# A two-stage mixer kernel on one core: second weights' high parts on ScalarE, a third staging buffer with loads two ahead, sums in pieces, first norm transposes later

## The chip, the cores and the metric

The kernel runs on 1 core of a Trainium2 chip. The metric is the device time of one execution in microseconds, lower is better.

## The reference

Per head (8 x 8 heads, 576 rows, 64 columns) an attention without scores: softmax of q along its columns, softmax of k along the rows, `kv = k_s^T v`, `q_s kv`. The heads are put side by side to x [8, 576, 512]. Then two stages:

```
u   = x + (relu(x^T w_tok1) w_tok2)^T          # mixing along the rows
x1  = u + relu(u w_ch1) w_ch2                  # w_ch1 512x1536
xn  = (x1 - mean) / sqrt(var + 1e-6) * g_ln    # per row
out = x1 + relu(xn w2_ch1) w2_ch2              # w2_ch1 512x2048
```

The weights come in as 64-bit floats; the kernel takes them as pairs of 32-bit words and decodes them on the chip.

## The kernel before, in words

**Precision.** Each operand of a large matmul is split into a high part (rounded to fp32r) and a low part, and each product is three matmuls (`PASSES`: high-high, high-low, low-high).

**Blocks.** The 4608 rows are nine blocks of 512 (`NB`). Blocks 0 to 7 are the first 512 rows of each batch entry; block 8 gathers the remaining 64 rows of each (the row ends), which go through `u_dram` (`load_ends`, L641). Phase 1 (`Phase1`, L647) computes x1 block by block: twelve steps `f` of 128 hidden columns, each `L1` (12 matmuls into `ph`, L675), the relu split (`relu_split`, L140: high part on ScalarE, low part on VectorE) and, two steps later (`LAG`), `L2` (12 matmuls into the accumulators `acc`, L692). Phase 2 (`Phase2`, L800) does the same for the normalised rows with sixteen steps (L814, L829). There are two `ph` buffers.

**Order of the work.** It is written out by hand. `later(n, fn)` (L308) puts a function n ticks ahead, `tick()` (L311) issues what is due. In phase 1 a step has four ticks (in the middle and at the end of L1 and of L2), in phase 2 two. Within an engine's queue the order is that of issue.

- Attention units (`Unit`, L401) of the next batch entry run beside phase 1 of blocks 2 to 6, each unit 10 ticks after the one before. POOL does the subtractions of k and q, the scaling of q and the low part of q (`q_split`, L507, tile `qn`), which `tok1` (L533, tile `pg`) multiplies.
- At a block's end `Phase1.finish` (L699) adds acc and the high part of u on VectorE (L713) and the low part of u on POOL, one instruction over the whole tile yT (L715). `y_store` (L619) transposes a quarter of it (tile `py`, L622) 5, 7, 9 and 11 ticks later, copies it on ScalarE (L632) and stores it to `y_dram` from ScalarE's DMA queue.
- `Norm(j)` (L728) loads a block of y from `y_dram` (`load_y`, L722, SP queue; its tile shares a buffer with that of the y stores), takes statistics (L753), normalises (`hat`, L778) and from 12 ticks on transposes (`turn`, tile `px`, L789) into xT. `Norm(0)` starts at tick 18 of block 8 of phase 1, `Norm(1)` at tick 14 of block 0 of phase 2.

**Weights.** `Loads` (L259) holds chunks of 512 KB, a load (SP queue) and a use. `decode` (L87) gives the use's steps: `rebias` (L100), `shift` (L108), `sign` (L115), `low` (L121), all on VectorE for the second weights (`late`), then `parts`: the high part by a copy on VectorE (L129) and the low part by a subtraction on POOL (L130). `pump` issues so many of these steps; the load of a later chunk stands between the `parts` of one chunk and the `rebias` of the next. The last argument but one of `Loads` is how many chunks are loaded ahead. The 32 chunks of the second weights start with block 7 of phase 1 (eight chunks, into the pool `w2pool`, which takes the place of the attention's tiles) and run on to the last steps of block 0 of phase 2, whose step f needs chunks up to 4(f // 2) + 2 and, for L2, + 4. They come through two staging buffers, given out by `stage` (L148): an entry of -1 in `extra` is one of the two main buffers, another the entry of `bufs`.

Of the kernel before, what the change touches and what calls it, by code (L numbers as in the profile page):

```python
# [8 lines left out]
F32 = mybir.dt.float32  # L9
# [15 lines left out]
def kernel(  # L25
# [61 lines left out]
    def decode(st, w, hi, lo):  # L87


        rows, n = st.shape[0], st.shape[1]  # L90
        w0, w1 = st[:, :, 0], st[:, :, 1]
        wf = w1.bitcast(F32)
        vec, late = nc.vector, bool(w2p)
        box = {}
        if late:
            box["t"] = main.tile([P, 512], U32, tag="t", bufs=2, name="t")[:rows, 0:n]

        def rebias():
            if late:
                vec.tensor_scalar(out=wf, in0=wf, scalar1=REBIAS, scalar2=None, op0=ALU.mult)  # L100
            else:
                nc.scalar.activation(out=wf, in_=wf, func=AF.Copy, scale=REBIAS)

        def shift():
            if not late:

                box["t"] = psum("dt").bitcast(U32)[:rows, 0:n]
            vec.tensor_scalar(  # L108
                out=box["t"], in0=w1, scalar1=3, scalar2=0x7FFFFFF8,
                op0=ALU.logical_shift_left, op1=ALU.bitwise_and,  # L110
            )

        def sign():
            t = box["t"]
            vec.scalar_tensor_tensor(  # L115
                out=t, in0=w1, scalar=0x80000000, in1=t, op0=ALU.bitwise_and, op1=ALU.bitwise_or
            )

        def low():
            t = box["t"]  # L120
            vec.scalar_tensor_tensor(  # L121
                out=t if late else w0, in0=w0, scalar=29, in1=t,
                op0=ALU.logical_shift_right, op1=ALU.bitwise_or,
            )

        def parts():
            x = w((box["t"] if late else w0).bitcast(F32))
            if late:
                vec.tensor_copy(out=hi, in_=x)  # L129
                nc.gpsimd.tensor_tensor(out=lo, in0=x, in1=hi.bitcast(F32), op=ALU.subtract)  # L130
            else:
                split(x, hi, lo, nc.gpsimd)

        return [rebias, shift, sign, low, parts]
# [173 lines left out]
    def later(n, fn):  # L308
        ticks.setdefault(now[0] + n, []).append(fn)
# [91 lines left out]
    class Unit:  # L401
# [7 lines left out]
        def start(self, at):  # L409
            steps = (  # L410
                self.k_max, self.k_top, self.q_max, self.q_sub, self.k_sub, self.q_exp,
                self.q_norm, self.k_exp, self.q_split, self.kv, self.tok1,
                lambda: self.q_T(0), self.hidden, lambda: self.q_T(1),
                lambda: self.tok2(0), lambda: self.tok2(1),
            )
            if self.n == 0:
                later(at + 10, lambda: loads.until(3))
                later(at + 14, lambda: loads.until(len(tok)))
            if self.early:
                when = (0, 1, 1, 1, 3, 3, 4, 5, 7, 8, 10, 10, 11, 12, 14, 15)  # L420
            else:
                when = (0, 2, 1, 2, 4, 4, 5, 6, 8, 8, 10, 11, 13, 12, 15, 16)
            for n, fn in zip(when, steps):
                later(at + n, fn)
# [194 lines left out]
    def y_store(j, c):  # L619
        pt = psum("py")  # L620
        for kk in range(KD):
            nc.tensor.transpose(  # L622
                out=pt[:, kk * P:(kk + 1) * P], in_=yT_t[j][:, kk, c * P:(c + 1) * P],
                identity=ident,
            )
        if w2p:
            if c == 0:
                yn_t[j] = w2p[0].tile([P, CT, DM], F32, tag="y", name="yn")
            yn = yn_t[j][:, c]
        else:  # L630
            yn = main.tile([P, DM], F32, tag="t", bufs=2, name="yn")
        nc.scalar.activation(out=yn, in_=pt[:, 0:DM], func=AF.Copy)  # L632
        if j < B:
            dst = y_dram[j * S:j * S + S0, :].rearrange("(p c) d -> c p d", c=NC)[c]
            nc.scalar.dma_start(out=dst, in_=yn)
            return
        for i in range(P // R):
            b = c * (P // R) + i
            nc.scalar.dma_start(out=y_dram[b * S + S0:(b + 1) * S, :], in_=yn[i * R:(i + 1) * R])
# [7 lines left out]
    class Phase1:  # L647
# [51 lines left out]
        def finish(self):  # L699
            if self.f1 < NF1:  # L700
                t = [main.tile([P, 512], F32, tag="t", bufs=2, name="part") for _ in range(2)]
                x = att.tile([P, 2, 512], F32, tag="qx", name="part")
                for dd, o in enumerate((t[0], t[1], x[:, 0], x[:, 1])):
                    nc.scalar.activation(out=o, in_=self.acc[dd], func=AF.Copy)
                for dd in range(2):
                    nc.sync.dma_start(out=part_dram[:, dd], in_=t[dd])
                nc.sync.dma_start(out=part_dram[:, 2:4], in_=x)
                return
            yT_t[self.j] = main.tile([P, KD, BLK], F32, tag="y", bufs=1, name="yT")
            yT, u = yT_t[self.j], u_t[self.j]  # L710
            for dd in range(KD):
                x = self.part[dd // 2][:, dd % 2] if self.f0 else u[:, 0, dd].bitcast(F32)
                nc.vector.tensor_tensor(out=yT[:, dd], in0=self.acc[dd], in1=x, op=ALU.add)  # L713
            if self.f0 == 0:
                nc.gpsimd.tensor_tensor(out=yT, in0=yT, in1=u[:, 1].bitcast(F32), op=ALU.add)  # L715
            for c in range(CT):
                later(5 + 2 * c, lambda c=c: y_store(self.j, c))


# [8 lines left out]
    class Norm:  # L728
        def __init__(self, j):
            self.j = j  # L730

        def start(self, at):
            def call(fn, i):
                return lambda: fn(i)

            later(at, self.load)
            for i in range(CT // 2):
                later(at + 4 + i, call(self.stats, i))
                later(at + 9 + i, call(self.hat, i))
            later(at + 6, self.root)  # L740
            later(at + 8, self.rstd)
            for kk in range(KD):
                later(at + 12 + kk + kk // 2, call(self.turn, kk))

        def load(self):
            self.y = load_y(self.j, w2p[0])
# [99 lines left out]
    with tc.manual_schedule():  # L846
# [89 lines left out]
        for o, f in steps:  # L936
            if isinstance(o, Phase1):
                if o.j == 1 and f == NF1 - 2:
                    for hp in range(NHP):
                        Unit(2 * NHP + hp).start(OFF + 1 + hp * GAP)  # L940
                    later(7, part.load_part)
                if f == 0:
                    if 1 < o.j < B - 1:
                        for hp in range(NHP):
                            Unit((o.j + 1) * NHP + hp).start(OFF + hp * GAP)
                    elif o.j == B - 1:
                        att.release()
                        w2pool = tc.alloc_tile_pool(name="w2pool", bufs=1, reuse_waits="tile")
                        pool_bufs[w2pool] = 4
                        w2p.append(w2pool)  # L950
                        extra.clear()
                        loads = Loads([
                            x
                            for g in range(NF2 // 2)
                            for x in ch_chunks(
                                wa2, w2_ch1, wb2, w2_ch2, g, w2pool if g < 2 else main
                            )
                        ], 1, 1, 8)
                        for n in range(5, 29):
                            later(n, lambda: loads.pump(2))  # L960
                        later(10, load_ends)
                    elif o.j == NB - 1:
                        Norm(0).start(18)
                if o.j <= 1:
                    loads.until(len(tok) + 4 * (f // 2) + 2)
            else:
                if o.j == 0:
                    loads.until(4 * (f // 2) + 2)
                if f == 0:
                    later(16, o.load)  # L970
                    if o.j + 1 < NB:
                        Norm(o.j + 1).start(14 if o.j == 0 else 8)
            ps, n = o.L1(f, tick)
            h = main.tile([P, 2, 512], F32R, tag="h", bufs=LAG + 1, name="h")
            relu_split(ps, h[:, 0, 0:n], h[:, 1, 0:n])
            tick()
            loads.pump(rate(7, 2, 3))
            pend.append((o, f, h))
            if len(pend) > LAG:
                do_L2()  # L980
                loads.pump(rate(4, 3, 4))
                tick()
# [34 lines left out]
```

## Time and profile before

| | |
|---|---|
| median of 3 runs | 1693.29 us (1693.03 to 1695.51) |
| the profiled execution | 1692.61 us, its span 1690.8 us |
| granted TensorE clock, mean | 0.998 of full speed |
| TensorE busy (matmuls) | 1650.4 us, 98% |
| VectorE busy | 665.7 us, 39% |
| ScalarE busy | 393.8 us, 23% |
| POOL busy | 314.2 us, 19% |

How to read it: times in the trace count from the start of the span. A row of the timeline has start, duration, engine, line, operation, output and inputs, how many instructions are merged, and in brackets the idle time before and what ended it. Phase 1 reaches block 7 near 726 us and block 8 near 800 us, phase 2 starts at 868 us. ACT is ScalarE, DVE VectorE, PE TensorE, POOL GpSimd, SPq the DMA queue of SyncE.

### The profile page before, as it was taken

The page shows a single profiled execution, that of the slowest core. Times are in us where ns is not written, and L with a number is a line of the kernel's source. Part 1 is how long each engine was busy: PE and PEld are TensorE (multiplying, and loading weights), DVE is VectorE, ACT ScalarE, POOL GpSimd, SP SyncE. Part 2 cuts the span into 40 slices and gives each one's busy share as a digit, 9 for nine tenths or more (in the row PEclk, how much of TensorE's full clock was granted, in tenths as well). Part 3 has the DMA queues.
Part 4 walks back from the last instruction along what each step waited for, and adds up shares of the span by engine and source line. Part 5 has one row for each costly group of instructions (what it writes and reads, how often), then busy time and mean ns, then how long its engine had stood idle before and what let it go on. Part 6 is the DMA issues. An engine that isn't in the chain of part 4 may idle for free.

```text
span 1690.8 us, 20156 instructions
## 1 busy us (share of the span) xinstructions
PE 1650.4 (98%) x8136; PEld 1379.6 (82%) x8136; DVE 665.7 (39%) x1322; ACT 393.8 (23%) x792; POOL 314.2 (19%) x220
## 2 busy tenths in 40 slices
PE   5999999999999999999999899999999999999998
PEld 4888888888888888888788788888888888888887
DVE  6875434343433434354567722222213122222211
ACT  4663323333232323311211111111111111111110
POOL 5744522232222313221222200000000000000000
PEclk9999999999999999999999999999999999999999
DMA  8452312122121212042225310101010102010010
GB/s 228 124 169 67 98 33 74 43 56 50 38 67 30 71 38 74 21 144 63 88 63 174 100 51 25 50 25 50 25 51 25 50 1 75 1 53 23 0 50 25
DMA packets 122062, 105.39 MB, mean 62 GB/s; under 512 B 92976, under 2 KB 101424, under 8 KB 118512
## 3 DMA queue, kind: packets, MB, share of 16 engines
q1 hardware_dynamic: 115568, 86.27, 17.6%
q10 hardware_dynamic: 5248, 9.44, 1.6%
q0 software_dynamic: 1152, 8.39, 1.2%
q8 instruction: 64, 1.05, 0.3%
q14 instruction: 30, 0.25, 0.0%
HBM read 82.05 MB, written 22.02 MB: 62 GB/s over the span
## 4 chain that ended last, share of the span: by engine, by line
PE 57%; DVE 3%; DMA 1%; POOL 0%; issue 0%; ACT 0%; SPq 0%; ACTq 0%; DVEq 0%
PE ph L814 22%; PE acc L829 22%; PE acc L692 5%; PE ph L675 5%; PE px L789 1%; DMA st<-in_moe_w_ch 1%; PE pu L592 1%; PE py L622 0%; PE pg L538 0%; DVE t L115 0%; DVE t L121 0%; POOL yT L715 0%; DVE t L108 0%; DMA y<-y_dram 0%; DVE y L778 0%; DMA y_dram<-yn 0%
## 5 line engine op out<-in xcount | busy, mean ns | idle before, releaser
L142 DVE SCALAR_TENSOR_TENSOR h<-ph,h 128x512 fp32r<-128x512 f32 x252 | 174.1, 691 | 687.9 <-ACT h L141 687.8
L814 PE MATMUL ph<-xT,w 128*128 128x512 f32 x1728 | 420.9, 392 | 2.3 <-DVE h L142 1.0
L829 PE MATMUL acc<-w,h 128*128 128x512 f32 x1728 | 420.0, 392 | 0.0
L814 PEld LDWEIGHTS ph<-xT,w 128*128 128x128 f32 x1728 | 322.8, 188 | 73.8 <-DVE h L142 1.6
L829 PEld LDWEIGHTS acc<-w,h 128*128 128x128 f32 x1728 | 323.0, 188 | 68.8
L141 ACT ACTIVATE h<-ph 128x512 fp32r<-128x512 f32 x252 | 150.8, 598 | 858.7 <-PE ph L814 636.3
L692 PE MATMUL acc<-h,w 128*128 128x512 f32 x1296 | 328.7, 396 | 0.0
L675 PE MATMUL ph<-u,w 128*128 128x512 f32 x1296 | 327.7, 396 | 0.0
L675 PEld LDWEIGHTS ph<-u,w 128*128 128x128 f32 x1296 | 236.2, 189 | 46.9 <-DVE u L612 0.4
L692 PEld LDWEIGHTS acc<-h,w 128*128 128x128 f32 x1296 | 236.2, 188 | 45.6
L844 POOL DMA_DIRECT2D out<-y x8 | 4.5, 558 | 637.4 <-DVE y L840 637.4
L467 POOL TENSOR_TENSOR qt<-rawq,qm 128x640 f32<-128x640 f32 x24 | 30.3, 1262 | 235.0 <-PE pt L461 153.7
L538 PE MATMUL pg<-w,qn 128*128 128x256 f32 x480 | 64.8, 286 | 6.4 <-ACT w L137 3.4
L538 PEld LDWEIGHTS pg<-w,qn 128*128 128x128 f32 x480 | 62.2, 193 | 9.8 <-POOL qn L138 3.9
L130 POOL TENSOR_TENSOR w<-t,w 128x512 fp32r<-128x512 f32 x32 | 42.9, 1341 | 130.8 <-DVE w L129 126.3
L592 PE MATMUL pu<-w,hs 128*128 128x288 f32 x384 | 61.4, 295 | 0.0
L592 PEld LDWEIGHTS pu<-w,hs 128*128 128x128 f32 x384 | 54.4, 188 | 0.3 <-ACT hs L141 0.2
L715 POOL TENSOR_TENSOR yT<-yT,u 128x2048 f32<-128x2048 f32 x8 | 37.2, 4648 | 69.8 <-DVE yT L713 65.6
L138 DVE TENSOR_TENSOR qT<-pq,qT 128x512 fp32r<-128x512 f32 (+1 forms) x48 | 21.8, 454 | 71.3 <-ACT qT L137 71.3
L482 POOL TENSOR_TENSOR kt<-rawk,kb 128x640 f32<-128x640 f32 x24 | 37.8, 1575 | 50.2 <-ACT kb L478 50.2
L138 POOL TENSOR_TENSOR qn<-qt,qn 128x640 fp32r<-128x640 f32 x24 | 38.2, 1591 | 41.7 <-ACT qn L137 41.7
L138 DVE TENSOR_TENSOR u<-pu,u 128x288 fp32r<-128x288 f32 x32 | 14.6, 455 | 67.8 <-ACT u L137 67.7
(132 smaller groups left out, 1256.3 us busy)
## 6 DMA issues: line engine op xcount, KB each, us to landing
st<-in_moe_w_ch SPq DMA_DIRECT2D x41, 512.0 KB, 3.7
y<-y_dram SPq DMA_DIRECT2D x18, 1024.0 KB, 4.8
vt<-in_v SPq DMA_DIRECT2D x64, 128.0 KB, 2.9
y_dram<-yn ACTq DMA_DIRECT2D x32, 256.0 KB, 2.4
out<-y POOLq DMA_DIRECT2D x8, 1024.0 KB, 4.1
rawk<-in_k SPq DMA_DIRECT2D x54, 128.0 KB, 2.7
rawq<-in_q SPq DMA_DIRECT2D x27, 256.0 KB, 3.0
stages<-in_moe_w_ch SPq DMA_DIRECT2D x9, 512.0 KB, 4.5
```

Source lines behind the costliest of these rows:

```text
L130: nc.gpsimd.tensor_tensor(out=lo, in0=x, in1=hi.bitcast(F32), op=ALU.subtract)
L138: engine.tensor_tensor(out=lo, in0=x, in1=hi.bitcast(F32), op=ALU.subtract)
L141: nc.scalar.activation(out=hi, in_=x, func=AF.Relu)
L142: nc.vector.scalar_tensor_tensor(out=lo, in0=x, scalar=0.0, in1=hi.bitcast(F32), op0=ALU.max, op1=ALU.subtract)
L482: nc.gpsimd.tensor_tensor(out=self.kt, in0=self.kr, in1=kb.to_broadcast([P, NC + 1, 2, D]), op=ALU.subtract,)
L538: nc.tensor.matmul(out=pg[:, 0:T], lhsT=self.qn[:, x, c], rhs=w1[:, y, c, :], start=(n == 0), stop=(n == len(terms) - 1),)
L592: nc.tensor.matmul(out=pu[:, 0:HN], lhsT=l, rhs=r, start=(n == 0), stop=(n == len(terms) - 1))
L675: nc.tensor.matmul(out=ps, lhsT=w[:, x, kk, fo:fo + P], rhs=u[:, y, kk], start=(n == 0), stop=(n == 3 * KD - 1),)
L692: nc.tensor.matmul(out=self.acc[dd], lhsT=w[:, x, f % 2, dd * P:(dd + 1) * P], rhs=h[:, y], start=(f == self.f0 and n == 0), stop=(f == se ...
L715: nc.gpsimd.tensor_tensor(out=yT, in0=yT, in1=u[:, 1].bitcast(F32), op=ALU.add)
L814: nc.tensor.matmul(out=ps, lhsT=w[:, x, kk, fo:fo + P], rhs=xT[:, y, kk], start=(n == 0), stop=(n == 3 * KD - 1),)
L829: nc.tensor.matmul(out=self.acc[c], lhsT=h[:, x, c * P:(c + 1) * P], rhs=w[:, y, f % 2], start=(f == 0 and n == 0), stop=(f == self.f1 - 1 ...
```

## The change

The high parts of the second weights are copied by ScalarE. The pool w2pool gets a third staging buffer (128 x 4 KB) as its first tile, `extra` gives the three out in turn, and the loads of the second weights run two chunks ahead. `load_ends` is issued 20 ticks into block 7 and not 10. The transposes of the first norm start 15 ticks after its load and not 12. The addition of the low part of u to yT is four instructions, one per 128 columns: in blocks 2 to 8 at 0, 2, 4 and 6 ticks after the block's end, in block 1 all at the next tick.

```diff
         def parts():
             x = w((box["t"] if late else w0).bitcast(F32))
             if late:
-                vec.tensor_copy(out=hi, in_=x)
+                nc.scalar.activation(out=hi, in_=x, func=AF.Copy)
                 nc.gpsimd.tensor_tensor(out=lo, in0=x, in1=hi.bitcast(F32), op=ALU.subtract)
...
-            if self.f0 == 0:
-                nc.gpsimd.tensor_tensor(out=yT, in0=yT, in1=u[:, 1].bitcast(F32), op=ALU.add)
+            def add(c):
+                x = slice(c * P, (c + 1) * P)
+                nc.gpsimd.tensor_tensor(
+                    out=yT[:, :, x], in0=yT[:, :, x], in1=u[:, 1, :, x].bitcast(F32), op=ALU.add
+                )
+
             for c in range(CT):
+                if self.f0 == 0:
+                    later(2 * c if self.j > 1 else 0, lambda c=c: add(c))
                 later(5 + 2 * c, lambda c=c: y_store(self.j, c))
...
-        def start(self, at):
+        def start(self, at, turns=12):
...
-                later(at + 12 + kk + kk // 2, call(self.turn, kk))
+                later(at + turns + kk + kk // 2, call(self.turn, kk))
...
-                        extra.clear()
+                        bufs[:] = [w2pool.tile([P, 512, 2], U32, name="stage3")]
+                        extra[:] = [-1, -1, 0]
...
-                        ], 1, 1, 8)
+                        ], 1, 2, 8)
                         for n in range(5, 29):
                             later(n, lambda: loads.pump(2))
-                        later(10, load_ends)
+                        later(20, load_ends)
                     elif o.j == NB - 1:
-                        Norm(0).start(18)
+                        Norm(0).start(18, 15)
```

## Rows read from the trace of the kernel before

**Rows 1.** The page, part 1: busy us, share of the span, instructions.

```profile
PE 1650.4 (98%) x8136; PEld 1379.6 (82%) x8136; DVE 665.7 (39%) x1322; ACT 393.8 (23%) x792; POOL 314.2 (19%) x220
```

**Rows 2.** Waits of TensorE, whole span: total us, times, longest.

```profile
PE pg L538 <- POOL qn L138: 3.1, 4, 0.8
...
PE px L789 <- DVE y L778: 1.8, 2, 1.1
...
PE ph L814 <- DVE h L142: 1.0, 1, 1.0
PE py L622 <- POOL yT L715: 0.9, 1, 0.9
PE ph L814 <- POOL w L130: 0.7, 1, 0.7
...
PE px L789 <- PE acc L692: 0.5, 1, 0.5
```

**Rows 3.** Windows of 20 us: busy us (instructions) per engine, clock, DMA share, GB/s.

```profile
740.00:760.00 20.00, 19.15 (x93) 15.61 (x92) 15.81 (x20) 4.20 (x7) 9.02 (x4) 1.00 0.67 235
840.00:860.00 20.00, 18.24 (x86) 14.46 (x85) 14.54 (x25) 3.85 (x6) 4.08 (x3) 1.00 0.25 79
...
920.00:940.00 20.00, 19.04 (x83) 14.98 (x81) 17.24 (x39) 1.89 (x4) 5.09 (x4) 1.00 0.51 178
940.00:960.00 20.00, 16.69 (x77) 12.79 (x77) 19.38 (x32) 4.45 (x7) 5.67 (x5) 1.00 0.39 119
```

**Rows 4.** Timeline of POOL, end of block 2.

```profile
358.98 4.59 POOL L715 TENSOR_TENSOR yT<-yT,u 128x2048 f32<-128x2048 f32 x1 [1.01 <-DVE yT L713]
363.52 1.64 POOL L138 TENSOR_TENSOR qn<-qt,qn 128x640 fp32r<-128x640 f32 x1
```

**Rows 5.** Timeline of SP's DMA queue, 902 to 916 us.

```profile
902.80 0.34 SPq L183 DMA_DIRECT2D st<-in_moe_w_ch  x1
915.29 0.34 SPq L725 DMA_DIRECT2D y<-y_dram  x1
915.68 0.42 SPq L183 DMA_DIRECT2D st<-in_moe_w_ch  x1
```

**Rows 6.** Timeline of VectorE, 880 to 941 us.

```profile
880.95 4.98 DVE L115 SCALAR_TENSOR_TENSOR t<-st,t 128x512 uint32<-128x512 uint32 x1
...
890.86 0.43 DVE L129 CAST w<-t 128x512 fp32r<-128x512 f32 x1
...
907.10 0.43 DVE L129 CAST w<-t 128x512 fp32r<-128x512 f32 x1
...
921.37 0.43 DVE L100 TENSOR_SCALAR st<-st 128x512 f32<-128x512 f32 x1 [8.67 <-DMA st<-in_moe_w_ch]
...
924.16 0.68 DVE L142 SCALAR_TENSOR_TENSOR h<-ph,h 128x512 fp32r<-128x512 f32 x1
...
940.45 0.99 DVE L778 TENSOR_SCALAR y<-y,mv,r 128x512 f32<-128x512 f32 x2
```

**Rows 7.** Lines by form (VectorE from 820 us, ScalarE, POOL): busy us, mean ns.

```profile
L129 DVE CAST w<-t 128x512 fp32r<-128x512 f32 x24 | 10.2, 425 | 0.7
...
L137 ACT ACTIVATE w<-st 128x512 fp32r<-128x512 f32 x11 | 7.9, 716 | 7.0 <-DVE st L121 7.0
...
L664 POOL TENSOR_TENSOR st<-st,u 128x512 f32<-128x512 f32 x8 | 10.3, 1295 | 4.3 <-DMA st<-part_dram 4.3
```

**Rows 8.** Chain that ended last, phase 2: start us, us, what.

```profile
1158.81 2.80 PE acc L829 x12
...
1200.09 2.72 PE ph L814 x12
```

**Rows 9.** Timeline of ScalarE, 917 us.

```profile
916.96 0.60 ACT L141 ACTIVATE h<-ph 128x512 fp32r<-128x512 f32 x1 [4.82 <-PE ph L814]
```

## The prediction

> **What bounds the kernel now.** The page comes first. TensorE is busy for 98% of the span and VectorE for 39% [rows 1], so only time in which TensorE stands still can be won, at most about 40 us. The list of waits of TensorE says where it stands [rows 2]. The reader should see that beyond the first 100 us (loading and the first attention units, which the change does not touch) few waits are left: pg for the low part qn on POOL, four times 0.8 us; py for the sum yT on POOL, once 0.9; px for the normalised y, twice, 1.8 together; and two kinds of ph waits. Then the busy time by stretches [rows 3]: 740 to 760 misses 0.85 us of 20, 840 to 860 misses 1.76, 920 to 940 misses 0.96 and 940 to 960 misses 3.31. With the four pg waits (3.1) this is 3.1 + 0.85 + 1.76 + 4.27 = 9.98 us. That is the pool from which the change can draw.
>
> Each has its own cause. (a) The sum over the whole yT block holds POOL for 4.59 us from 358.98, and qn starts only at 363.52, when it ends [rows 4]; this pattern comes four times, once in each block with attention beside it. (b) The wait at 740 is py behind the same sum in block 7, which no attention follows. (c) At 840 the first norm's px stands at its place in the order of ticks before y is ready. (d) Around 920 to 960 the SP queue is the start. It issues a weight load at 902.80 and nothing more until 915.29, when the y load of the second norm goes out; the next weight load stands behind it and goes at 915.68 [rows 5]. VectorE runs dry, waits 8.67 us for that load until 921.37, and is late from then on: the normalising of y starts at 940.45 [rows 6], and px and ph wait for it in the following stretch.
>
> **The change part by part.**
>
> *Sums in pieces.* One POOL instruction per block becomes four. The nearest row is the addition of a 128x512 tile on POOL, 1.295 us [rows 7], so four cost 5.2 us where one cost 4.59; POOL is not a bound, so the 0.6 more costs nothing as long as its queue stays ahead. For blocks 2 to 8 the pieces go out 0, 2, 4 and 6 ticks after the end of the block, and the split of the second attention unit falls between piece 0 and piece 1. So qn waits for 1.3 us of sum and not for 4.6: it starts about 3.3 us sooner than 363.52, and the pg wait of 0.8 ends. Gain: 3.1 us over four blocks. Queued behind the pieces are k and q steps of the next unit; piece 3 goes in behind that unit's q subtraction, and the buffer of u that it frees is written by ScalarE some three ticks later, so I cost it at nothing; without that cover ScalarE would wait by up to one piece, 1.3 us, in each of four blocks. In block 7 the first py needs piece 0 alone, ready 1.3 us and not 4.6 after the sums of VectorE: the 0.85 goes. Block 1 has all four pieces at once, one tick later than the whole sum; a 128x512 addition of the part sums gets in front. Between 0.6 us lost and 0.2 won; I take 0.
>
> *First norm's transposes three ticks later.* A tick in phase 1 is half of a group of 12 matmuls, 2.72 / 2 = 1.36 us [rows 8]; three are 4.1 us, against 1.76 of waiting. The four px groups still end 11 ticks ahead of the block's end, where phase 2 needs them. Of the 1.76 I take 1.3, since one px wait of 0.5 is put down to the matmuls of acc and not to y [rows 2]. Norm 0 alone is moved; its load, statistics and their DMA keep their place.
>
> *High parts on ScalarE.* It removes 32 casts of 0.425 us from VectorE and gives ScalarE 32 copies; the early weights show the same copy there at 0.716 us [rows 7]. ScalarE is busy 23% of the span [rows 1], so 23 us more is hidden. POOL's low part now waits for ScalarE, 0.3 us later than before. What is queued behind a copy is the relu of the next hidden tile: a copy waits for VectorE's fourth decoding step, so a VectorE that is late now makes ScalarE late too. The relu's other half is on VectorE in any case, behind the same steps: a relu finished at 916.96 + 0.60 got its VectorE half only at 924.16 [rows 6, 9], so I cost this wait at nothing as long as the lag stays under what the two ph buffers cover, about 5.5 us, and at 0.72 per chunk beyond it.
>
> *Third buffer, two ahead.* The loads keep their places in the order but each now fetches the chunk after the one it fetched before. So the weight load ahead of the y load carries the chunk that VectorE had to wait for from 912 to 921. VectorE needs 4.06 us a chunk (casts at 890.86 and 907.10 are four chunks apart [rows 6]), less 0.43 for the cast: it decodes one chunk more inside the gap. It reaches the second norm's normalising about 3.6 us (that chunk) + 4 x 0.43 (casts of the four chunks between) = 5.3 us sooner, at 935 where 940.45 stood. TensorE found y late by 1.1 us at the longest and had 1.0 of ph stall before that [rows 2], so without stalls it wants y some 2 us sooner than it came, about 938.5. So both waits on y, the ph wait on h, and the one for the last weights go: 4.27 us. The gap itself stays, since the y load still waits for the four y stores; behind it three weight chunks and two y blocks are now in flight, not two and two, so the last lands later, by some 2 us at the pace of these rows (915.68 to 921.37 for the first chunk behind y). That comes off a lead of 5.3, not off TensorE. *The load of the row ends* goes from tick 10 to 20, behind eight weight chunks and not three; it is needed some 28 ticks on, 38 us, and SP has nothing urgent behind it: 0.
>
> *A rule weighed.* One of VectorE's decoding steps took 4.98 us at 880.95, beside a yT sum on POOL, longer than a whole chunk [rows 6]. The Trainium skill, "SBUF — State Buffer", section "Who interferes with whom", says that a VectorE instruction with two SBUF inputs and a reading GpSimd instruction exclude each other for a whole instruction. By that rule cutting the sum gives VectorE nothing back, since four holds add up to one, and the row agrees as to the hold; it leaves the next sums as they are, and lowers only the lead in (d). The lead in the sum above has no gain from the pieces; if VectorE loses 5.2 instead of 4.6 us to them, 4.7 us of it are left.
>
> *Not shown in the trace:* the buffer is 4 KB per partition in front of the four weight tiles of the late pool, whose groups of 12 matmuls take 2.80 us where the others take 2.72 [rows 8]. Eight groups in each of nine blocks are 72 x 0.08 = 5.8 us. If moving the tiles ends that, 5.8 us are won; as much may be lost if it worsens. The order and size of the tiles stay, so I take 0 and keep both ends.
>
> **Sum.** 3.1 + 0.85 + 1.3 + 4.27 = 9.5 us. The profiled execution took 1692.61 us (span 1690.8, 1.8 around it); it would take 1683.1. The median of the three runs is 0.68 above it: 1683.8. About 0.2%, 3.4 us, is what a measurement can tell from no change.
>
> **Rivals.** *VectorE stays the bound around 940* (13%): the gap behind the y load only moves by a chunk, and landing times of three chunks at once eat the lead. For it: VectorE was busy 19.38 us of 20 from 940 to 960 [rows 3]. Against it: 5.3 us of lead. Then 3.1 + 0.85 + 1.3 = 5.3 are won: 1688.0. *The change does less than it says* (8%): piece 1 or the split's own inputs still keep qn behind, and (d) stays; then 0.85 + 1.3, about 2 us, are won: 1691.2. Against it: in [rows 4] qn waits for nothing else after 363.5. *The tiles' place* (4%): the slow groups become fast, 9.5 + 5.8: 1678.0. *Slower* (5%): ScalarE's copy, VectorE's decoding and the relu become one chain. From the point where the fourth step is later than the relu by more than a step of 5.5 us, each of some 16 chunks between 878 and 957 puts 0.72 + 0.60 into the path of ph, 21 us, against 9.5 won: 1705. The rows for it are the relu and its VectorE half 6.6 us behind [rows 6, 9]; against it, that lag came out of the gap, which now holds a chunk's work.
>
> **How the numbers follow.** The forecast has 70%. Faster by over 0.2%: forecast, first rival and tiles, 0.87; same: 0.08; slower: 0.05. The range leaves out the slower case, the tiles and most of the smallest gain: from 1680.5 (the 0.5 not taken, the spread of the runs, and a part of the tiles) to 1688.5 (first rival).
>
> **What would show it.** In the waits of TensorE no pg behind qn after 300 us and no py behind yT; in the stretches 740 to 960 TensorE busy 20 of 20; on SP one more weight load ahead of the y load near 915; the wait of VectorE there for y or for a chunk one further; its normalising near 935. Wrong would be a wait of ph for ScalarE, a px wait left near 940, or groups of 12 matmuls at another pace in phase 2.

## The result and the profile after

| | before | changed |
|---|---|---|
| median | 1693.69 us (4 runs, 1693.03 to 1695.51) | 1680.03 us (4 runs, 1679.30 to 1680.36) |
| ratio, 95% interval | | 0.9917 (0.9900 to 0.9934) |
| profiled execution, its span | 1692.61, 1690.8 us | 1680.36, 1678.6 us |
| TensorE busy | 1650.4 us | 1646.2 us |

The changed kernel is 13.7 us faster. That is the forecast's direction, but 3.8 us beyond its value (1683.8) and half a microsecond below its range (1680.5 to 1688.5).

Waits of TensorE in the changed kernel from 190 us on (total us, times, longest), beside [rows 2]:

```profile
PE py L622 <- DVE qT L138: 0.5, 1, 0.5
PE py L622 <- POOL yT L716: 0.5, 1, 0.5
```

All pg, px and ph waits of that list are gone. One py wait on the sum is there, 0.5 us (further down it turns out to be at another py than before); the one on qT stood in the trace of before as well. The windows say the same, beside [rows 3]:

```profile
740.00:760.00 20.00, 19.49 (x94) 15.71 (x93) 15.95 (x19) 6.62 (x12) 12.08 (x9) 1.00 0.51 160
840.00:860.00 20.00, 20.00 (x98) 16.58 (x97) 11.56 (x21) 6.39 (x11) 3.87 (x3) 1.00 0.25 79
...
920.00:940.00 20.00, 20.00 (x94) 16.55 (x92) 18.27 (x34) 5.84 (x11) 5.76 (x5) 1.00 0.40 128
940.00:960.00 20.00, 20.00 (x93) 16.50 (x92) 10.58 (x17) 4.63 (x8) 3.89 (x3) 1.00 0.17 64
```

POOL at the end of block 2, beside [rows 4]: the split qn now stands behind one piece of the sum, and starts 1.8 us after the pieces begin and not 4.5.

```profile
359.96 1.27 POOL L716 TENSOR_TENSOR yT<-yT,u 128x512 f32<-128x512 f32 x1 [1.01 <-DVE yT L713]
361.79 1.58 POOL L138 TENSOR_TENSOR qn<-qt,qn 128x640 fp32r<-128x640 f32 x1 [0.56 <-ACT qn L137]
```

SP's queue and VectorE around the second norm, beside [rows 5] and [rows 6]. The queue is blocked as before, from 896.7 to 909.7, behind the y load.

```profile
896.38 0.34 SPq L183 DMA_DIRECT2D stage<-in_moe_w_ch  x1
909.73 0.33 SPq L731 DMA_DIRECT2D y<-y_dram  x1
```

```profile
906.47 0.42 DVE L100 TENSOR_SCALAR stage<-stage 128x512 f32<-128x512 f32 x1
...
914.57 1.29 DVE L759 BATCH_NORM_STATS2 st<-y 128x6 f32<-128x512 f32 x2 [2.10 <-DMA y<-y_dram]
...
928.35 1.99 DVE L784 TENSOR_SCALAR y<-y,mv,r 128x512 f32<-128x512 f32 x2
```

VectorE decodes the chunk in the third buffer (906.47) while the queue is blocked. Its long wait (8.67 us, for a chunk) has shrunk to 2.1 us, and is for y now. The normalising comes 12.1 us sooner than in [rows 6]; 5.8 us of that had been won before that stretch began.

The lines that the change made, beside [rows 7]: the copy on ScalarE takes 0.633 us where 0.716 was assumed, a piece of the sum on POOL 1.358 where 1.295 was.

```profile
L129 ACT ACTIVATE w<-t 128x512 fp32r<-128x512 f32 x32 | 20.3, 633 | 94.0 <-DVE t L121 91.7 <-DVE t L108 1.2 <-DVE st L100 1.2
```

```profile
L716 POOL TENSOR_TENSOR yT<-yT,u 128x512 f32<-128x512 f32 x32 | 43.0, 1358 | 37.7 <-DVE yT L713 37.6
```

**Where the time went.** ScalarE's relu (h, L141) comes once a step in either kernel, so the difference between the starts of the same step's relu shows what was won up to there. The first and the last, of before and then of the changed kernel:

```profile
97.27 0.60 ACT L141 ACTIVATE h<-ph 128x512 fp32r<-128x512 f32 x1 [2.29 <-PE ph L675]
...
1678.18 0.60 ACT L141 ACTIVATE h<-ph 128x512 fp32r<-128x512 f32 x1 [4.84 <-PE ph L814]
```

```profile
98.66 0.60 ACT L141 ACTIVATE h<-ph 128x512 fp32r<-128x512 f32 x1 [2.29 <-PE ph L675]
...
1666.25 0.60 ACT L141 ACTIVATE h<-ph 128x512 fp32r<-128x512 f32 x1 [4.84 <-PE ph L820]
```

The changed kernel's profile lost 1.4 us in the start, which it does not touch, and won 1580.91 - 1567.59 = 13.3 us from there on. By the same differences, stretch by stretch:

| stretch | gaps in the trace of before | forecast | won |
|---|---|---|---|
| four blocks with attention | 3.1 | 3.1 | 4.2 (1.02 to 1.07 each) |
| block 7, py | 0.85 | 0.85 | 0.2 |
| first norm, px | 1.76 | 1.3 | 2.55 |
| 920 to 960, px and ph | 4.27 | 4.27 | 6.2 |

With 0.4 at block 1 and some tenths either way between, this is the 13.3. In three of four places more was won than the trace of before shows as gaps.

### The profile page after: what moved, and what is told of

The parts are those of the page before. It is cut to its first block, busy times and chain, and to the rows that moved or that the text cites. A ratio compares the mean times of both kernels' runs of the same rounds, so it can differ in the third digit from the quotient of the medians.

```text
span 1678.6 us, 20194 instructions
## 1 busy us (share of the span) xinstructions
PE 1646.2 (98%) x8136; PEld 1378.8 (82%) x8136; DVE 642.6 (38%) x1290; ACT 411.4 (25%) x824; POOL 318.8 (19%) x244
## 3 DMA queue, kind: packets, MB, share of 16 engines
q8 instruction: 64, 1.05, 0.3%
## 4 chain that ended last, share of the span: by engine, by line
PE 93%; DVE 2%; POOL 1%; issue 1%; DMA 1%; SPq 1%; ACT 1%; POOLq 0%; ACTq 0%; DVEq 0%
PE ph L820 24%; PE acc L835 23%; PE ph L675 17%; PE acc L692 17%; PE pu L592 4%; PE pg L538 3%; PE pk L514 2%; PE px L795 1%; PE py L622 1%; PE ph L577 1%; PE pq L555 1%; DMA rawq<-in_q 0%; PE pt L461 0%; DVE spare L138 0%; POOL w L138 0%
## 5 line engine op out<-in xcount | busy, mean ns | idle before, releaser
L141 ACT ACTIVATE h<-ph 128x512 fp32r<-128x512 f32 x252 | 150.5, 597 | 767.2 <-PE ph L820 589.8
L716 POOL TENSOR_TENSOR yT<-yT,u 128x512 f32<-128x512 f32 x32 | 43.0, 1358 | 37.7 <-DVE yT L713 37.6
L129 ACT ACTIVATE w<-t 128x512 fp32r<-128x512 f32 x32 | 20.3, 633 | 94.0 <-DVE t L121 91.7
```

The source lines that it names most:

```text
L141: nc.scalar.activation(out=hi, in_=x, func=AF.Relu)
L716: nc.gpsimd.tensor_tensor(out=yT[:, :, x], in0=yT[:, :, x], in1=u[:, 1, :, x].bitcast(F32), op=ALU.add)
```

## The experiments

**Each part alone, on the kernel before.** Four runs; the diffs are the change's own, each without the others (the sums take the later `load_ends` with them).

```diff
# e1_sums: the sums in pieces, load_ends at 20
# e2_turns
-                        Norm(0).start(18)
+                        Norm(0).start(18, 15)
# e3_buffer
-                        extra.clear()
+                        bufs[:] = [w2pool.tile([P, 512, 2], U32, name="stage3")]
+                        extra[:] = [-1, -1, 0]
-                        ], 1, 1, 8)
+                        ], 1, 2, 8)
# e4_act
-                vec.tensor_copy(out=hi, in_=x)
+                nc.scalar.activation(out=hi, in_=x, func=AF.Copy)
```

> The kernel before with the sums in pieces alone (and the load of the row ends at tick 20, which the pieces need). Theory S: a stall of TensorE costs its gap in the trace and some 0.3 us more that the trace books as busy matmuls; then the four pg stalls are worth 4 x 1.05 = 4.2 us, with block 7 and the block before the four some 0.2 to 0.6 more: 4.4 to 5 us, and between one block and the next the lead grows by 1.05. Theory G: a stall costs its gap alone, and what was won beyond the forecast comes from somewhere else (the start, another pace of the matmuls): 3.1 us, 0.77 per block, and up to 0.85 in block 7. Both expect no pg wait on POOL.

> The kernel before with the first norm's transposes three ticks later alone. Theory S: 2.5 us are won by the end of block 8, as in the changed kernel, where the trace of before shows 1.76 of gaps. Theory G: 1.3 to 1.8 us. If the transposes cost nothing of the sort and the 2.5 came from the loads two ahead, under 1 us.

> The kernel before with the third staging buffer and the loads two ahead alone; the high parts stay on VectorE. If the chunk that is decoded in the gap behind the y load is what ends the stalls from 920 to 960: the normalising of the second norm some 3.6 us sooner, 4 to 6 us won (theory S for the stalls: 6.2, theory G: 4.3). If it takes the casts off VectorE as well: under half of that, with px or ph waits left from 930 to 960.

> The kernel before with the high parts on ScalarE alone; two buffers, one ahead. The wait of VectorE for a weight chunk behind the y load stays (8 us or more); it is 0.43 sooner per chunk behind it, some 1.7 at the second norm. If the buffer is what ends the stalls: 1 to 2.5 us won, px and ph waits left. If the casts are: 4 us or more. The rival of a chain over ScalarE (relu held by a copy, 0.72 + 0.60 a chunk): slower than before, with ph waits for ScalarE.

| | median us | ratio to before (1693.11) |
|---|---|---|
| sums in pieces | 1690.20 | 0.9982 (0.9972 to 0.9992) |
| transposes later | 1690.31 | 0.9980 (0.9970 to 0.9989) |
| buffer, two ahead | 1689.29 | 0.9973 (0.9962 to 0.9984) |
| high parts on ScalarE | 1691.91 | 0.9988 (0.9979 to 0.9998) |

*Sums.* By the relu times 4.4 us are won up to block 7, 1.05 in each of the four blocks: theory S's figure, not G's 0.77. In block 7 nothing is won (0.1 is lost): its py wait is 0.9 us as before. Then 1.2 us are lost again between 914 and 980. There the stalls of before stay, from 920 to 940 TensorE is busy for 16.09 of 20 us, and in the next window its clock falls as well. The third figure from the end of that window's row is the granted clock, a mean of 0.92 of full speed, where the same window of before stood at 1.00 [rows 3]: part of it ran at 1.2 GHz and not at 2.4. One group of 12 matmuls takes 4.48 us, where others show 2.9 to 3.0:

```profile
940.00:960.00 20.00, 19.90 (x87) 16.04 (x87) 18.72 (x30) 4.00 (x7) 5.80 (x5) 0.92 0.39 132
```

```profile
937.89 0.74 PE L795 MATMUL px<-ident,y 128*128 128x128 f32 x2 [0.98 <-PE ph L820]
939.36 0.93 PE L795 MATMUL px<-ident,y 128*128 128x128 f32 x2 [0.73 <-DVE y L784]
939.94 4.48 PE L835 MATMUL acc<-w,h 128*128 128x512 f32 x12
```

*Transposes.* 2.6 us by the relu times at the end of block 8, where 1.76 stood as gaps: theory S, and independent of the loads. Behind that nothing more is won: the gaps from 920 to 960 are 1.5 us shorter than before, but the window from 940 to 960 has a clock of 0.91.

*Buffer.* The normalising starts 3.5 us sooner (936.91 against 940.45), as the forecast's one chunk. The stretch from 860 to 980 wins 4.9 us by the relu times, more than G's 4.3 and less than S's 6.2, and 0.7 of gaps remain at 940 to 960. It lost 1.6 us ahead of that, where its profile has a clock of 0.91 around the first norm's stall. *ScalarE.* VectorE waits 9.02 us for the chunk behind the y load, and the px and ph waits stay: 1.2 us are won. Nothing there waits for ScalarE, so the rival of a chain is out. The two ph waits for w are gone as well; the window from 940 to 960 has a clock of 0.91.

One by one the parts win 0.8%, 10.7 us by the medians; together they win 13.7. Each of the four profiles has one window with a clock of 0.91 or 0.92, an estimated 1.6 to 1.8 us, so each part alone shows less than it is worth; how much of the 3 us between the two sums this makes was not measured.

**One part taken out of the change.** `e7_one_ahead` has two buffers and depth 1 again, `e6_dve_cast` the cast on VectorE again (the diffs above, reversed).

> The changed kernel with two buffers and one chunk ahead again; casts on ScalarE. If the buffer is what ends the stalls from 920 to 960: 3 to 5 us slower than the changed kernel, px and ph waits back. If the casts are enough: within 1 us of the changed kernel.

> The changed kernel with the high parts on VectorE again; three buffers, two ahead. If the buffer carries part (d) and the copies on ScalarE add nothing there: within 1 us of the changed kernel, with at most a short ph or px wait between 920 and 960. If the casts are needed beside it: 1.5 to 4 us slower, with px or ph waits back in that stretch.

Without the buffer 1684.93 us (ratio to before 0.9948, 0.9933 to 0.9963): 4.9 us of the gain are gone. Some of this is clock: the profiled execution, 1685.96 us and the slowest of the four, has 0.92 in the window from 920 to 940, and the fastest took 1684.23. The long wait of VectorE is back, and with it these waits of TensorE:

```profile
915.31 0.43 DVE L100 TENSOR_SCALAR st<-st 128x512 f32<-128x512 f32 x1 [10.05 <-DMA st<-in_moe_w_ch]
```

```profile
PE ph L820 <- DVE h L142: 1.7, 1, 1.7
PE px L795 <- PE ph L820: 0.9, 1, 0.9
PE px L795 <- DVE y L784: 0.7, 1, 0.7
```

With the casts on VectorE 1681.72 us (0.9927, 0.9912 to 0.9942), 1.7 us behind the changed kernel by the medians. The two intervals overlap, so the times alone don't show that the casts matter; the waits do:

```profile
PE py L622 <- POOL yT L716: 0.9, 1, 0.9
PE ph L820 <- POOL w L130: 0.7, 1, 0.7
PE ph L820 <- DVE w L129: 0.6, 1, 0.6
PE px L795 <- DVE y L784: 0.5, 1, 0.5
```

So the third buffer, with the loads two ahead, carries the stretch from 920 to 960, but not alone: with the casts back on VectorE (0.43 us a chunk), the weights of the last steps (w) still come 1.3 us late and y 0.5. Buffer and depth were only changed together.

**What a stall costs.** Two kernels add the same work to 48 steps of phase 2: two transposes on TensorE and a 128x128 copy on ScalarE. In the second kernel the second transpose reads the copy.

```diff
+                if isinstance(o, Phase2) and 2 <= o.j < 5:
+                    p0, p1 = psum("p0"), psum("p1")
+                    nc.tensor.transpose(out=p0[:, 0:P], in_=ident, identity=ident)
+                    nc.scalar.activation(out=probe[0], in_=p0[:, 0:P], func=AF.Copy)
+                    # e5a_probe_free: in_=ident; e5b_probe_wait: in_=probe[0]
+                    nc.tensor.transpose(out=p1[:, 0:P], in_=ident, identity=ident)
```

> The changed kernel with, after each of the 48 steps of blocks 2 to 4 of phase 2, two more transposes on TensorE and a 128x128 copy on ScalarE, of which TensorE waits for none. Both theories: longer than the changed kernel by 96 transposes, some 96 x 0.11 = 10.5 us, no gap on TensorE. It is the other half of the next run.

> The same, but the second transpose reads what ScalarE copied, so TensorE stands still 48 times. The spans of the two differ by what 48 stalls cost; the trace shows the gaps. Theory S: the difference is the gaps and 48 x 0.3 = 14 us more. Theory G: the difference is the sum of the gaps.

1697.48 and 1724.36 us (8 and 2 runs): 26.9 apart. The waits of TensorE in that stretch, first kernel and second:

```profile
PE p L996 <- ACT probe L995: 5.0, 6, 0.8
```

```profile
PE p L996 <- ACT probe L995: 22.9, 48, 0.8
```

The first was expected to have no gap and has six, 5.0 us; so 42 more stalls add 17.9 us of gaps and cost 26.9 us: 0.64 us each, of which the trace shows 0.43 as a gap and books 0.21 as busy. Theory S holds, with 0.21 here where 0.3 was expected. The trace of the pg stall at the end of block 2 shows where it hides. Before:

```profile
363.12 1.34 PE L538 MATMUL pg<-w,qn 128*128 128x256 f32 x10
365.21 0.86 PE L538 MATMUL pg<-w,qn 128*128 128x256 f32 x5 [0.76 <-POOL qn L138]
365.91 1.55 PE L675 MATMUL ph<-u,w 128*128 128x512 f32 x6
```

And the changed kernel:

```profile
364.09 1.93 PE L538 MATMUL pg<-w,qn 128*128 128x256 f32 x15
365.86 1.55 PE L675 MATMUL ph<-u,w 128*128 128x512 f32 x6
```

From the first pg matmul to the ph group it is 2.79 us before and 1.77 after: 1.02 us for a gap of 0.76. Ten matmuls and five, each run to their end, show 1.34 + 0.86 = 2.20 us busy; fifteen without a break show 1.93. The last matmul before a gap and the first behind it do not overlap with a neighbour.

The px waits of the second norm show the same. Before:

```profile
937.17 2.88 PE L814 MATMUL ph<-xT,w 128*128 128x512 f32 x12
941.08 0.74 PE L789 MATMUL px<-ident,y 128*128 128x128 f32 x2 [1.03 <-issue]
942.55 0.78 PE L789 MATMUL px<-ident,y 128*128 128x128 f32 x2 [0.72 <-DVE y L778]
943.09 3.01 PE L829 MATMUL acc<-w,h 128*128 128x512 f32 x12
```

And the changed kernel:

```profile
929.98 2.89 PE L820 MATMUL ph<-xT,w 128*128 128x512 f32 x12
932.71 0.60 PE L795 MATMUL px<-ident,y 128*128 128x128 f32 x4
933.07 3.00 PE L835 MATMUL acc<-w,h 128*128 128x512 f32 x12
```

From the ph group to the acc group it is 5.92 us before and 3.09 after: 2.83 us for two gaps of 1.75 together. The clock is 1.00 in these windows of both kernels, so none of this is clock.

**The place of the late pool's tiles.** The prediction left open why groups that read weights from the late pool take 2.80 us [rows 8]. In the changed kernel they still do, though the tiles lie 4 KB further on. The pool starts at a multiple of 64 bytes within a partition, while all large tiles of the main pool (weights, xT, u, h) start 32 bytes beyond one.

```diff
# e8_pad: 8 words; e10_pad64: 16 words
+                        w2pool.tile([P, 8], U32, name="pad")
                         bufs[:] = [w2pool.tile([P, 512, 2], U32, name="stage3")]
# e11_all_64: the above with 8 words, and ahead of the main pool's large tiles
+    main.tile([P, 8], U32, name="mainpad")
```

> The changed kernel with an unused tile of 32 bytes per partition in front of the third buffer: the tiles of the late pool then start at 32 beyond a multiple of 64 bytes, as those of the main pool do. If the place within 64 bytes is why 72 groups of 12 matmuls take 2.80 us and the others 2.72: all groups of phase 2 at 2.72 and about 5 us faster than the changed kernel. If it is which part of the memory they lie in: no difference.

> The changed kernel with 64 bytes of padding and not 32: the late pool's tiles lie elsewhere, but at the same place within 64 bytes as without it. If the place within 64 bytes counts: the 72 slow groups stay at 2.80 us and the time is that of the changed kernel. If any other shift does as well: as fast as with 32 bytes.

> The changed kernel with 32 bytes of padding in the main pool and in the late pool, so that the weights of both, xT, u and h all start at a multiple of 64 bytes. If a matmul is slow when its two operands lie at different places within 64 bytes: all groups at 2.72, some 7 us faster than the changed kernel. If a start at a multiple of 64 bytes is itself slow: all groups of phase 1 and 2 at 2.80 or more, some 504 - 72 = 432 groups x 0.08 = 35 us slower than the changed kernel.

| | late pool, main pool (bytes beyond a multiple of 64) | median us | ratio to before (1694.03) |
|---|---|---|---|
| changed kernel | 0, 32 | 1680.03 | 0.9917 (0.9900 to 0.9934), before 1693.69 |
| 32 bytes | 32, 32 | 1673.09 | 0.9877 (0.9860 to 0.9893) |
| 64 bytes | 0, 32 | 1679.83 | 0.9917 (0.9902 to 0.9932) |
| both pools | 0, 0 | 1673.96 | 0.9882 (0.9865 to 0.9898) |

The chain in block 3 of phase 2 (start us, us, what) with 64 bytes, with 32, and with both pools at multiples of 64:

```profile
1148.81 2.79 PE ph L820 x12
1151.60 2.80 PE acc L835 x12
```

```profile
1148.99 2.72 PE acc L835 x12
1151.71 2.72 PE ph L820 x12
```

```profile
1147.14 2.72 PE ph L821 x12
1149.86 2.72 PE acc L836 x12
```

It is not a start at a multiple of 64 that is slow, nor that part of the memory: these matmuls are slow when their two operands lie at different places within 64 bytes. Only the places 0 and 32 were tried. The expectation of 35 us lost with both pools at multiples of 64 is out.

**A faster version.** The 32 bytes, and the first piece of each sum issued at once:

```diff
-                if self.f0 == 0:
+                if self.f0 == 0 and self.j > 1 and c == 0:
+                    add(c)
+                elif self.f0 == 0:
                     later(2 * c if self.j > 1 else 0, lambda c=c: add(c))
```

> The changed kernel with the 32 bytes of padding, and the first piece of each sum issued at once at the block's end and not at the next tick, so that in block 7 it stands ahead of POOL's low part. The py wait on POOL in block 7 (0.5 us) goes: 0.5 to 0.8 us faster than with the padding alone, if a stall costs its gap and 0.2 to 0.3 more; 0.5 if the gap alone.

1672.42 us, ratio 0.9874 (0.9859 to 0.9889): 21 us below before. That it beats the padding alone (1673.09) the times can't tell; the trace has the py wait in block 7 down from 0.5 to 0.2 us and 0.4 us won at that place. That wait is at the fourth py, behind the last piece of the sum, and not at the first, which waits in neither kernel. POOL, and TensorE's wait, in the changed kernel:

```profile
750.14 1.29 POOL L130 TENSOR_TENSOR w<-t,w 128x512 fp32r<-128x512 f32 x1 [1.35 <-ACT w L129]
751.39 1.73 POOL L716 TENSOR_TENSOR yT<-yT,u 128x512 f32<-128x512 f32 x1
```

```profile
753.17 0.66 PE L622 MATMUL py<-ident,yT 128*128 128x128 f32 x4 [0.51 <-POOL yT L716]
```

And in this one:

```profile
748.28 1.30 POOL L130 TENSOR_TENSOR w<-t,w 128x512 fp32r<-128x512 f32 x1 [1.36 <-ACT w L129]
749.54 1.73 POOL L716 TENSOR_TENSOR yT<-yT,u 128x512 f32<-128x512 f32 x1
```

```profile
751.33 0.66 PE L622 MATMUL py<-ident,yT 128*128 128x128 f32 x4 [0.18 <-POOL yT L716]
```

## Why the prediction was right and where it was wrong

*What bounds the kernel, and the four causes* were right but for half of (b): the pg, px and ph waits named are gone in the profile after, and with each part alone went those put down to it (sums: pg; transposes: the two px waits of the first norm; buffer: the stretch from 920, but for 0.7 us at w). One reading in (d) was wrong: the 1.1 us by which "TensorE found y late" are the first norm's wait; at the second norm it is 1.03 and 0.72, as the px lines above show. The lead was long enough for that too.

*The step that failed is the sum, "3.1 + 0.85 + 1.3 + 4.27".* It prices every stall at its gap in the trace, and a stall costs more: 0.64 us for 0.43 of gap in the pair of probes, 1.02 for 0.76 at pg, 2.83 for 1.75 at the second norm's px. Measured, the terms are 4.2 + 0.2 + 2.55 + 6.2, and 0.4 at block 1. The 4.2 of the four blocks are explained in full by the 1.02. At 920 to 960 the excess over the gaps is 1.9 us; 1.08 of it is at the two px waits, the rest at the ph wait and the two waits for w. At the first norm 0.8 is excess over three gaps (1.06 and 0.45 in the list of waits, 0.25 more in the window); that it arises in the same way is argued and was not tried by itself. The 0.5 taken off there for a wait "put down to the matmuls of acc" was wrong: that wait went too, with the transposes alone.

*Sums in pieces, block 7.* The forecast was 0.85; 0.2 came. "The first py needs piece 0 alone" was right, and the first py no longer waits. What was overlooked is the last piece: POOL runs it behind the low part of a weight chunk, which itself waits for the copy of its high part (750.14 and 751.39 above), and the fourth py waits 0.51 us for it. With the copies on VectorE that wait is 0.9, so the sums alone won nothing there. *Block 1* was taken at 0 and gave 0.4, where the prediction had 0.2 as its good case: the addition of the part sums came in front, and a short wait for kt (0.16 us) went.

*High parts on ScalarE.* Hidden, as costed: from 190 us on no wait of TensorE names ScalarE, though ScalarE's copies idle 91.7 us for VectorE's fourth step. That they were counted only as 0.43 a chunk of lead was right in size; that without them TensorE would still wait 1.8 us for w and y was not seen.

*Third buffer, two ahead.* Right in mechanism and size: the blocked queue stays, one chunk more is decoded inside it, the lead over before is 940.45 - 5.8 - 928.35 = 6.3 us, and 5.3 was worked out. The rival that VectorE stays the bound around 940 describes the changed kernel without the casts or without the buffer, not the whole.

*The rule weighed.* The prediction let the cut of the sum give VectorE nothing. The Trainium skill, "SBUF — State Buffer", section "Who interferes with whom", has a VectorE instruction with two SBUF inputs and a reading GpSimd instruction exclude each other. The profile after agrees as to the hold: VectorE's third step beside a POOL instruction (897.09 to 898.38) takes 1.68 us, without one 0.69; the 4.98 of [rows 6] doesn't come again. But "four holds add up to one" did not come out: with the sums alone VectorE is busy for 657.3 us, where it was 665.7. The copies on ScalarE, on the other hand, lengthen that step (mean 0.982 us with them alone, 0.825 before). No wait of TensorE in the changed kernel from 190 us on hangs on either.

```profile
897.25 1.68 DVE L115 SCALAR_TENSOR_TENSOR t<-st,t 128x512 uint32<-128x512 uint32 x1
...
907.46 0.69 DVE L115 SCALAR_TENSOR_TENSOR t<-stage,t 128x512 uint32<-128x512 uint32 x1
```

*The tiles' place* was kept at 0 with both ends open. The change itself moved nothing there, as 4 KB is a multiple of 64 bytes; the 5.8 us worked out for it were there to be had by other means, 7 us by the medians.

## What to carry to other kernels

In these traces a gap of TensorE is less than the stall costs: add some 0.2 to 0.3 us per stall (0.5 at the px waits), and price many short stalls by their number as well as by their sum. Follow every piece of work that is cut up, the last one too: a wait can move from the first to the last. Where loads share a queue with one that must wait, a buffer more lets a load pass ahead of it; count how many chunks stand in front of the blocked one. When groups of equal matmuls run at two paces, compare the start addresses of their operands before looking at any engine.

## What the runs showed that was not expected

Two operands of a 128x128x512 fp32r matmul at different places within 64 bytes cost 0.08 us in 12 (2.80 against 2.72), in groups that follow each other without a gap. The Trainium skill, "SBUF — State Buffer", section "Who interferes with whom", gives TensorE two read ports that are independent of each other; these runs show that the pace still depends on where the two operands start.

Stalls can cost clock as well. The profiles of five of the kernels with stalls left between 840 and 960 have a granted clock of 0.91 or 0.92 in one of those windows of 20 us; taken as lost time, an estimate from these rows, that is 20 x 0.09 = 1.8 us. The profile of before has the same stalls and no such window, and 48 short stalls in a row (the second probe) had none either, so what brings it on stays open. The medians hold some of it: of 48 executions of the kernel before beside these experiments, the 14 with a mean clock of 0.997 took 1693.7 to 1695.4 us, the 7 with 0.999 or 1.000 1692.1 to 1694.1. So a part of the 13.7 us, which these rows do not size, may be clock; the 13.3 us by the relu times are not, since between 97 and 1660 us neither profile has a window below 1.00.
